# A third exponential chain on the job bank, and the last query block's products begun early, in a fused attention and token-mixing kernel

## The chip, the cores and the metric

The kernel runs on one core of one Trainium2 chip. The metric is the device time in microseconds (us) of one execution. A profiled execution also gives the span from the first to the last instruction, which is about 2 us shorter than the device time, and the mean granted clock of TensorE (1.0 is full speed).

## The reference

```python
x  = A_x                                   # (1, 2048, 640) bf16
xn = layernorm(x)
# multi-head attention: 32 heads of 20, wqkv 640 x 1920, wo 640 x 640
q, k, v = split(xn @ wqkv)
s = concat(softmax(q k^T * 20**-0.5) v) @ wo
# token-mixing MLP over the sequence: F = 1536
u = gelu(einsum("bsd,sf->bdf", layernorm(xn), w1) + b1)
y = (einsum("bdf,fs->bds", u, w2) + b2).transpose(0, 2, 1)
return x + s * silu(y)
```

## The kernel before

The kernel's Python is a planner. It keeps a clock for each engine, with its own estimates of every instruction and transfer, and at each step emits the candidate instruction that it ranks best. What reaches the chip is one fixed order of instructions for each engine, tied together by semaphores.

The softmax is 2048 units of 128x512 scores, which TensorE writes into PSUM banks. ScalarE takes pairs of units from banks (0,1) and (2,3). VectorE takes single units from banks 4 and 5, each with a chain of six instructions. Bank 6 accumulates the value products. Bank 7 is the job bank: QKV, the MLP and the output products pass through it one after the other.

TensorE has slack, and the kernel fills it (797.6 of 865.0 us busy, of which 68.0 us are recorded filler). Filler matmuls go to the job bank when that is empty (`warm_step`), or with zero weights into the accumulator (`warm_acc`). They are there for the sake of TensorE's granted clock. The planner wants at least `WARM_FLOOR` columns of matmul in a window of its own clock; the window's length, 3413 ns, is a constant of the program.

```python
    OP_FROM = (1792.0, 1852.0, 1926.0)   # from which unit on the products of query blocks 0..2 may start
    ACT_GROUPS = ((0, 1), (2, 3))
    DVE_GROUPS = ((4,), (5,))
    DVE_TAIL_GUARD = 3                   # VectorE keeps off the last units of a pass
    LAST_GUARD = 10
    WARM_ACC = 3600.0
    WARM_FLOOR = 3600.0
    QSPLIT = ((0, 256), (256, 256))      # the last pass comes in two halves
# ... class Prog
    DMA_LAT = 2000.0                     # what the planner takes a transfer to need, ns
    def dma(self, fn, ...):
        # ...
        t.fin = self.pipe = max(t.t0 + self.DMA_LAT, self.pipe) + nbytes / self.DMA_RATE
```

The output products need the heads' results transposed. They are stored to a scratch tensor in DRAM, and each query block is loaded back by a transposing load, `oT`. Before the change, the products of the last query block are released in this way (comments are mine):

```python
        for i, (q0, nq) in enumerate(self.QSPLIT[:-1]):
            b0, nb = NB - 4 + q0 // 128, nq // 128
            # epL0: the first half of the last pass has been accumulated and stored
            rq = oTall[NTB - 1] + ("wo", f"epL{i}") + tuple(f"a2_{b}" for b in range(b0, b0 + nb))
            for b in range(b0, b0 + nb):
                add_bank_job(f"op{b}_0", op_steps(b), rq, 30.0, NU - UP)
                add_job(f"res{b}", res_steps(b), (f"op{b}_0", f"op{b}_1", f"x2_{NTB - 1}"), 30.0)
            # ...
        BA, BB = (5, 7), (4, 0)          # fixed banks for the very last products
        def tail_fin(i):
            b = LBS[i]
            steps = op_mms(b, ps(BA[i]), 0, 512, bank_slot[BA[i]], False, True)
            steps += op_mms(b, ps(BB[i], 128), 512, 128, bank_slot[BB[i]], False, True)
            # ...
```

Of the kernel before, what the change touches and what calls it, by code (L numbers as in the profile page):

```python
# [7 lines left out]
ALU = mybir.AluOpType  # L8
# [274 lines left out]
class _Kern:  # L283
# [14 lines left out]
    DVE_GROUPS = ((4,), (5,))  # L298
# [10 lines left out]
    DVE_TAIL_GUARD = 3  # L309
    LAST_GUARD = 10  # L310
    NTMP = 4
# [90 lines left out]
    def schedule(self):  # L402
# [785 lines left out]
        def emit_dchain(chn):  # L1188
            (fn, rd, wr, cost), us, s0, grp = chn.pop(0)
            tk = pr.dve(fn, reads=rd, writes=wr, name=f"dexp{us[0]}", cost=cost)  # L1190
            if not chn:
                dchains.remove(chn)
                dgrp_state[grp] = "free"
                for i, u in enumerate(us):
                    avail.append((tk.fin, u, "d", s0 + i))
# [253 lines left out]
        for i, (q0, nq) in enumerate(self.QSPLIT[:-1]):  # L1449
            b0, nb = NB - 4 + q0 // 128, nq // 128  # L1450
            rq = oTall[NTB - 1] + ("wo", f"epL{i}") + tuple(f"a2_{b}" for b in range(b0, b0 + nb))
            for b in range(b0, b0 + nb):
                add_bank_job(f"op{b}_0", op_steps(b), rq, 30.0, NU - UP)
# [4 lines left out]
        BA, BB = (5, 7), (4, 0)  # L1458

        def tail_fin(i):  # L1460
            b = LBS[i]
            steps = op_mms(b, ps(BA[i]), 0, 512, bank_slot[BA[i]], False, True)
            steps += op_mms(b, ps(BB[i], 128), 512, 128, bank_slot[BB[i]], False, True)
            z = ztmp(i)
            g = regC[:, b, :]
            steps.append(("act", lambda e: e.activation(z[:, 512:640], ps(BB[i], 128), AF.Copy), [bank_slot[BB[i]]],
                          [S_(f"z{i}_1")], f"tz{b}b", ac(128)))
            if i == 0:
                steps.append(("dve", lambda e: e.tensor_tensor(g[:, 0:512], ps(BA[i]), g[:, 0:512], ALU.mult),
                              [bank_slot[BA[i]], S_(f"g{b}")], [S_(f"r{b}_0")], f"tp{b}a", dv(512)))  # L1470
                steps.append(("dve", lambda e: e.tensor_tensor(g[:, 512:640], z[:, 512:640], g[:, 512:640], ALU.mult),
                              [S_(f"z{i}_1"), S_(f"g{b}")], [S_(f"r{b}_1")], f"tp{b}b", dv(128, .52)))
            else:
                steps.append(("act", lambda e: e.activation(z[:, 0:512], ps(BA[i]), AF.Copy), [bank_slot[BA[i]]],
# [9 lines left out]
        for i, b in enumerate(LBS):  # L1484
            rq = oTall[NTB - 1] + ("wo", f"a2_{b}")
            add_job(f"tpa{i}", (lambda bk, i=i, b=b: op_mms(b, ps(BA[i]), 0, 512, bank_slot[BA[i]], True, False) + [
                ("tag", f"tpa{i}")]), rq + (f"bankoff{BA[i]}",), 60.0 + i)
            add_job(f"tpb{i}", (lambda bk, i=i, b=b: op_mms(b, ps(BB[i], 128), 512, 128, bank_slot[BB[i]], True, False) + [
                ("tag", f"tpb{i}")]), rq + (f"bankoff{BB[i]}",), 60.0 + i)
            add_job(f"tfin{i}", (lambda bk, i=i: tail_fin(i)),  # L1490
                    (f"tpa{i}", f"tpb{i}", f"epL{len(self.QSPLIT) - 1}", f"x2_{NTB - 1}"), 10.0 + i)


# [16 lines left out]
        def pe_cands(T):  # L1510
            c = []
            if nxt[0] < NU and unit_ok(nxt[0]):
# [3 lines left out]
                for gi in range(len(self.ACT_GROUPS)):  # L1516
                    grp = self.ACT_GROUPS[(last_grp[0] + 1 + gi) % len(self.ACT_GROUPS)]
                    if grp_state[grp] == "free" and all(fin_bank(b) for b in grp):
# [3 lines left out]
                        while len(us) < n and u < NU and unit_ok(u):  # L1522
                            us.append(u)
                            u += 1
                            while u in taken:
                                u += 1
                        if len(us) < n and u < NU:
# [6 lines left out]
            if dveready[0] and self.DVE_EXP:  # L1534
                for dg in self.DVE_GROUPS:
                    if dgrp_state[dg] == "free" and all(fin_bank(b) for b in dg) and dg[0] not in bank_off and dve_room(dg):
# [22 lines left out]
            if self.WARM:  # L1559
                wb = warm_bank()  # L1560
                if wb is None and acc_ok[0] and pv_pass[0] < LASTP and pr.gate.warm \
                        and (pv_left[0] == UP or all(pv_seen.get((pv_pass[0], g), NB) < NB for g in range(GH))):
# [16 lines left out]
            for j in active:  # L1579
                s = j.steps[j.i]  # L1580
                if s[0] == "pe":
                    c.append((j.prio if pr.gate.warm or not self.WARM else -2.0, pr.ready("pe", s[2], s[3]),
# [24 lines left out]

        def dve_room(dg):
            return dve_pick(dg) is not None

        def take_dve(dg, rows=()):
# [4 lines left out]
            dgrp_state[dg] = "full"  # L1616
            dexp.append((du, dg, dg))
# [6 lines left out]
        def do_st(grp, us):  # L1624
# [9 lines left out]
            if self.DVE_EXP and dveready[0]:  # L1634
                for dg in self.DVE_GROUPS:
                    rows = {units[u][3] for u in lst}
                    if dgrp_state[dg] == "free" and len(lst) + len(dg) <= 4 and all(fin_bank(b) for b in dg) \
                            and dg[0] not in bank_off and dve_pick(dg, rows) is not None \
# [5 lines left out]
        def do_step(j, eng):  # L1644
            s = j.steps[j.i]
            j.i += 1
            if s[0] == "ev":
                n = s[8]
                fn = ev_fn(s, eng)
                cost = ac(n) if eng == "act" else dv(n, 0.55 if s[7].startswith("xTe") else 1.04)  # L1650
                getattr(pr, eng)(fn, reads=s[5], writes=s[6], name=s[7], cost=cost)
# [48 lines left out]
        def warm_acc():  # L1700

            zero = bass.AP(v_sb, voff(H - 1) + 22, [[NB * VB, P], [0, P]])
            new = pv_left[0] == UP
            pe_full(lambda e: e.matmul(ps(AB), zero, wrm_sb[:, P:P + 512], start=new, stop=new),  # L1704
# [100 lines left out]
```

## Time and profile before

Three runs gave 866.85 us (866.6 to 866.88). The prediction shows the busy shares and the groups. Beside them:

| what | before |
|---|---|
| units on ScalarE / VectorE | 1776 / 272 |
| filler matmuls, by their weight loads | 263 (214 have a record of their own, 68.0 us busy) |
| VectorE started later than 80 ns before the previous record's end, 60 to 765 us, summed | 41.0 us |
| end of the last exponential | 855.4 us |
| from there to the end of the span | 9.6 us |
| span of a run with full clock | 865.0 us |

Some matmul records are missing from this trace: it has 5918 weight loads (PEld) and 5828 matmuls. The filler lines have 130 and 133 weight loads for 117 and 97 matmuls.

The view by stretches of time is the one to read for the clock. Its columns are the stretch, its length, then the busy us and the instructions of PE, of PE's weight loads, of VectorE, ScalarE and GpSimd, then the granted clock of TensorE, the DMA share and GB/s. The kernel before:

```profile
765.00:815.00 50.00, 45.54 (x340) 13.55 (x344) 47.15 (x117) 49.94 (x56) 0.00 (x0) 1.00 0.32 86
815.00:850.00 35.00, 32.36 (x332) 12.75 (x337) 32.70 (x83) 35.00 (x39) 0.00 (x0) 1.00 0.15 34
850.00:869.00 19.00, 10.17 (x101) 4.08 (x95) 8.62 (x20) 6.42 (x9) 0.00 (x0) 0.95 0.11 37
```

ScalarE is busy all 35.00 us of the stretch from 815 to 850 us, and TensorE has its full clock (the 0.95 of the last row comes from a half clock that starts at 865.25 us, after the end of the span at 865.0).

### The profile page before, as it was taken

The page shows a single profiled execution, that of the slowest core. Times are in us where ns is not written, and L with a number is a line of the kernel's source. Part 1 is how long each engine was busy: PE and PEld are TensorE (multiplying, and loading weights), DVE is VectorE, ACT ScalarE, POOL GpSimd, SP SyncE. Part 2 cuts the span into 40 slices and gives each one's busy share as a digit, 9 for nine tenths or more (in the row PEclk, how much of TensorE's full clock was granted, in tenths as well). Part 3 has the DMA queues.
Part 4 walks back from the last instruction along what each step waited for, and adds up shares of the span by engine and source line. Part 5 has one row for each costly group of instructions (what it writes and reads, how often), then busy time and mean ns, then how long its engine had stood idle before and what let it go on. Part 6 is the DMA issues. An engine that isn't in the chain of part 4 may idle for free.

```text
span 865.0 us, 16498 instructions
## 1 busy us (share of the span) xinstructions
PE 797.6 (92%) x5828; PEld 256.1 (30%) x5918; DVE 823.6 (95%) x2047; ACT 845.4 (98%) x925; POOL 14.0 (2%) x23
## 2 busy tenths in 40 slices
PE   8899999999999999999999999999899998998997
PEld 5422222222222223222322222222222222232233
DVE  8989999999999999999999999999999999999996
ACT  7899999999999999999999999999999999999996
POOL 3200000000000000000000000000000000000000
PEclk9999999999999999999999999999999999999999
DMA  8141010011010323010013022123312201042111
GB/s 236 48 113 30 9 35 10 16 36 31 11 55 14 77 36 88 11 55 10 16 25 78 23 51 52 25 52 71 67 30 46 47 11 11 3 102 69 41 39 41
DMA packets 123350, 39.32 MB, mean 45 GB/s; under 512 B 84312, under 2 KB 122152, under 8 KB 123272
## 3 DMA queue, kind: packets, MB, share of 16 engines
q1 hardware_dynamic: 123272, 38.27, 19.4%
q8 instruction: 50, 0.82, 0.4%
q14 instruction: 28, 0.23, 0.1%
HBM read 25.88 MB, written 9.83 MB: 41 GB/s over the span
## 4 chain that ended last, share of the span: by engine, by line
ACT 87%; PE 9%; DVE 2%; POOL 1%; issue 1%; ACTq 0%; POOLq 0%
ACT pt_sb L1137 85%; PE ps_all L1109 3%; PE ps_all L1224 1%; ACT zt_sb L843 1%; PE ps_all L755 1%; PE ps_all L879 1%; ACT zt_sb L838 1%; PE ps_all L1704 1%; DVE ew_sb L1177 0%; PE ps_all L683 0%; PE ps_all L722 0%; POOL v_sb L1298 0%; PE ps_all L703 0%; DVE dpt_sb L1183 0%; PE ps_all L658 0%
## 5 line engine op out<-in xcount | busy, mean ns | idle before, releaser
L1137 ACT ACTIVATE pt_sb<-ps_all 128x1024 bf16<-128x1024 f32 x888 | 819.9, 1147 | 3.6 <-PE ps_all L1109 3.0
L1109 PE MATMUL ps_all<-qk_sb 32*128 32x512 bf16 (+1 forms) x2112 | 367.8, 377 | 48.3 <-ACT pt_sb L1137 36.7
L1177 DVE TENSOR_SCALAR ew_sb<-ps_all 128x512 uint16<-128x512 uint16 x272 | 184.2, 684 | 20.7 <-PE ps_all L1109 19.6
L1109 PEld LDWEIGHTS ps_all<-qk_sb 32*128 32x128 bf16 x2112 | 97.1, 91 | 347.0 <-ACT pt_sb L1137 299.9
L1183 DVE SCALAR_TENSOR_TENSOR dpt_sb<-ps_all,el_sb 128x512 uint16<-128x512 f32 x272 | 182.0, 684 | 1.8
L1224 PE MATMUL ps_all<-pt_sb,v_sb 128*32 128x512 bf16 (+1 forms) x1833 | 162.6, 378 | 0.3 <-issue 0.3
L1181 DVE TENSOR_TENSOR el_sb<-ev_sb,el_sb 128x512 bf16<-128x512 bf16 x272 | 111.0, 417 | 1.1
L1182 DVE TENSOR_TENSOR el_sb<-el_sb,ew_sb 128x512 bf16<-128x512 bf16 x272 | 110.2, 417 | 0.9
L1224 PE MATMUL ps_all<-dpt_sb,v_sb 128*32 128x512 bf16 (+1 forms) x279 | 83.7, 379 | 0.0
L810 PE MATMUL ps_all<-regB,regA 128*128 128x128 bf16 (+1 forms) x371 | 75.6, 300 | 2.9 <-issue 1.1
L1178 DVE TENSOR_SCALAR ev_sb<-ew_sb 128x512 bf16<-128x512 uint16 x272 | 75.3, 285 | 2.3
L810 PE MATMUL ps_all<-regC,regA 128*128 128x128 bf16 (+1 forms) x370 | 74.2, 300 | 1.8 <-issue 1.0
L1179 DVE TENSOR_SCALAR el_sb<-ew_sb 128x512 bf16<-128x512 uint16 x272 | 75.1, 284 | 0.0
L722 PE MATMUL ps_all<-xnT_sb,wqk_sb 128*112 128x512 bf16 x200 | 68.2, 405 | 0.4 <-DVE zt_sb L816 0.4
L1224 PEld LDWEIGHTS ps_all<-pt_sb,v_sb 128*32 128x32 bf16 x1833 | 35.4, 94 | 55.6 <-issue 50.2
L1696 PE MATMUL ps_all<-wrm_sb 128*128 128x512 bf16 (+1 forms) x117 | 34.0, 376 | 3.9 <-DVE ps_all L513 2.2
L810 PEld LDWEIGHTS ps_all<-regB,regA 128*128 128x128 bf16 x384 | 25.8, 97 | 39.1 <-issue 24.0
L810 PEld LDWEIGHTS ps_all<-regC,regA 128*128 128x128 bf16 x384 | 25.0, 97 | 39.8 <-issue 28.1
L1704 PE MATMUL ps_all<-wrm_sb,v_sb 128*128 128x512 bf16 x97 | 34.0, 385 | 1.3 <-issue 0.7
L755 PE MATMUL ps_all<-wv_sb,xnT_sb 128*128 128x160 bf16 (+1 forms) x160 | 33.7, 303 | 0.4 <-DVE pk_sb L1030 0.3
L879 PE MATMUL ps_all<-wo_sb,xnT_sb 128*128 128x128 bf16 (+3 forms) x151 | 30.2, 298 | 1.1 <-issue 0.5
L722 PEld LDWEIGHTS ps_all<-xnT_sb,wqk_sb 128*112 128x112 bf16 x200 | 20.7, 127 | 30.5 <-issue 13.4
(89 smaller groups left out, 354.4 us busy)
## 6 DMA issues: line engine op xcount, KB each, us to landing
regA<-in_B_w_dram SPq DMA_DIRECT2D x6, 1024.0 KB
regA<-in_B_w_dram SPq DMA_DIRECT2D x8, 768.0 KB
qkT_scratch_dram<-pk_sb SPq DMA_DIRECT2D x40, 112.0 KB
qk_sb<-qkT_scratch_dram SPq DMA_DIRECT2D x56, 80.0 KB
regA<-in_A_x_dram SPq DMA_DIRECT2D x6, 640.0 KB
on_scratch_dram<-on_sb SPq DMA_DIRECT2D x124, 20.0 KB
out_dram<-regC SPq DMA_DIRECT2D x3, 640.0 KB
wqk_sb<-in_A_wqkv_dram SPq DMA_DIRECT2D x2, 680.0 KB
```

The costliest lines, as they stand in the source:

```text
L722: steps.append(("pe", lambda e, dc=dc: e.matmul(ps_all[0:112, bk * 512:(bk + 1) * 512], wqk_sb[:, dc * 1280 + c0:dc * 1280 + c0 + 112], xn ...
L810: steps.append(("pe", lambda e, k=k: e.matmul(ps(bk, n), wap[:, k, col0:col0 + 128], rows[:, k, c0:c0 + n], start=(k == 0), stop=(k == nk ...
L1109: pr.pe(lambda e, outp=outp, lhsT=lhsT, rhs=rhs, g=g: e.matmul(outp, lhsT, rhs, start=True, stop=True, tile_position=(32 * g, 0)), reads=q ...
L1137: tk = pr.act(lambda e: e.activation(outp, inp, AF.Exp, bias=-self.OFFS * math.log(2.0) / 128.0, scale=math.log(2.0) / 128.0), reads=[bank ...
L1177: (lambda e: e.tensor_scalar(w3, lo, 0x7FFF, None, ALU.bitwise_and), bs, [sw], dv(N)),
L1178: (lambda e: e.tensor_scalar(v_, w_, 1.0 / 256.0, -128.0, ALU.mult, ALU.add), [sw], [sv], dv(N, .26)),
L1179: (lambda e: e.tensor_scalar(l_, w_, a3 / 65536.0, (b3 - 64.0 * a3) / 256.0, ALU.mult, ALU.add), [sw], [sl_], dv(N, .26)),
L1181: (lambda e: e.tensor_tensor(l_, v_, l_, ALU.mult), [sv, sl_], [sl_], dv(N, .52)),
L1182: (lambda e: e.tensor_tensor(l_, l_, w_, ALU.mult), [sl_, sw], [sl_], dv(N, .52)),
L1183: (lambda e: e.scalar_tensor_tensor(o_, zr, -(self.OFFS - 16256.0), l_, ALU.add, ALU.add), bs + [sl_], [S_(f"dpt{s0 + i}") for i in range( ...
L1224: pr.pe(lambda e, outp=outp, lhsT=lhsT, rhs=rhs, k=k, g=g: e.matmul(outp, lhsT, rhs, start=(k == 0), stop=(k == NB - 1), tile_position=(0, ...
L1704: pe_full(lambda e: e.matmul(ps(AB), zero, wrm_sb[:, P:P + 512], start=new, stop=new), [S_("warm"), S_("v_ones")], [sl_acc], "warmz", 512)
```

## The change

The intent has three parts. VectorE may run a third chain on the job bank while no job holds it. The first product of the last query block is split: its first part, over the heads that are done earlier, starts `EARLY = 42` units before the end, and its second part follows when the last heads are in. And the very last products take whichever bank comes free first, in place of four fixed ones. A few planner rules change with them. The core of the diff:

```diff
-    DVE_GROUPS = ((4,), (5,))
+    DVE_GROUPS = ((4,), (5,), (7,))
+    SHARED = (7,)
+    JOB_PRIO = 20.0
+    SHARE_END = 1780
...
-    DVE_TAIL_GUARD = 3
+    DVE_TAIL_GUARD = 12
+    EARLY = 42
...
+            def early(bk):
+                return op_mms(b0, ps(bk), 0, 512, bank_slot[bk], True, False) + [
+                    ("call", lambda: keep(bk)), ("tag", f"opA{b0}")]
...
+            def late(_):
+                bk = kept[1]
+                g = regC[:, b0, 0:512]
+                return op_mms(b0, ps(bk), 0, 512, bank_slot[bk], False, True) + [
...
+            add_bank_job(f"opA{b0}", early, oTall[NTB - 1] + ("wo",), 30.0, NU - self.EARLY)
+            add_job(f"opB{b0}", late, rq + (f"opA{b0}",), 11.0)
+            for b in range(b0 + 1, b0 + nb):
+                add_bank_job(f"op{b}_0", op_steps(b), rq, 30.0, NU - UP)
...
-        BA, BB = (5, 7), (4, 0)
+        tbank = []
...
+        def bank_out(b):
+            bank_off.add(b)
+            tbank.append(b)
+            done.add(f"tbank{len(tbank) - 1}")
...
+        def share_ok(dg):
+            return dg[0] not in self.SHARED or nxt[0] < self.SHARE_END
...
+                if s[3] in ("q", "k"):
+                    cost += 130.0
```

Left out here: the bookkeeping of the shared bank, the rule that a pair's two units come from different row groups, and the filler in the accumulator, which is now also allowed in the last passes.

## The prediction

> **What bounds the kernel now.** I read the page's first part, then its chain of waits, then the groups of instructions, then the timeline of VectorE. Busy shares come first.
>
> ```profile
> PE 797.6 (92%) x5828; PEld 256.1 (30%) x5918; DVE 823.6 (95%) x2047; ACT 845.4 (98%) x925; POOL 14.0 (2%) x23
> ACT 87%; PE 9%; DVE 2%; POOL 1%; issue 1%; ACTq 0%; POOLq 0%
> ```
>
> ScalarE is busy 98% of the span, and 87% of the chain that ended last runs through it. VectorE follows with 95%. The groups say what fills them (line, engine, operation, tiles, shapes, count | busy, mean ns | idle before):
>
> ```profile
> L1137 ACT ACTIVATE pt_sb<-ps_all 128x1024 bf16<-128x1024 f32 x888 | 819.9, 1147 | 3.6 <-PE ps_all L1109 3.0
> L1177 DVE TENSOR_SCALAR ew_sb<-ps_all 128x512 uint16<-128x512 uint16 x272 | 184.2, 684 | 20.7 <-PE ps_all L1109 19.6
> L1696 PE MATMUL ps_all<-wrm_sb 128*128 128x512 bf16 (+1 forms) x117 | 34.0, 376 | 3.9 <-DVE ps_all L513 2.2
> L1704 PE MATMUL ps_all<-wrm_sb,v_sb 128*128 128x512 bf16 x97 | 34.0, 385 | 1.3 <-issue 0.7
> ```
>
> The softmax has 32 heads x 4 query blocks x 16 key blocks = 2048 units of 128x512 scores. ScalarE exponentiates 888 x 2 = 1776 of them, two per instruction; VectorE does the other 272, each by a chain of six instructions. So the two engines share one pool of work, and the end comes when both have emptied it. Some of VectorE's idle time is a wait for scores: 20.7 us before the first instruction of a chain (L1177). TensorE isn't the bound: 34.0 + 34.0 us of its work are filler matmuls (L1696, L1704)[...].
>
> The timeline of VectorE alone shows the bubble (start, duration, line, count; idle before it in brackets):
>
> ```profile
> 379.17 1.28 DVE L1177 TENSOR_SCALAR ew_sb<-ps_all 128x512 uint16<-128x512 uint16 x2
> 380.37 0.48 DVE L1178 TENSOR_SCALAR ev_sb<-ew_sb 128x512 bf16<-128x512 uint16 x2
> 380.77 0.49 DVE L1179 TENSOR_SCALAR el_sb<-ew_sb 128x512 bf16<-128x512 uint16 x2
> ...
> 382.99 0.41 DVE L1182 TENSOR_TENSOR el_sb<-el_sb,ew_sb 128x512 bf16<-128x512 bf16 x1
> 383.32 0.74 DVE L816 TENSOR_SCALAR zt_sb<-ps_all,b1h_sb 128x512 bf16<-128x512 f32 x1
> ...
> 384.31 1.28 DVE L1183 SCALAR_TENSOR_TENSOR dpt_sb<-ps_all,el_sb 128x512 uint16<-128x512 f32 x2
> 386.34 1.29 DVE L1177 TENSOR_SCALAR ew_sb<-ps_all 128x512 uint16<-128x512 uint16 x2 [0.75 <-PE ps_all L1109]
> ```
>
> Both chains walk in step. They release their two PSUM banks together at 385.6 us, and VectorE stands for 0.75 us until TensorE has refilled one. A third chain is meant for this hole.
>
> [...] between 60 and 765 us that wait for scores comes 33 times, 14.0 us in all. [...] The kernel uses four for ScalarE, two for the chains, one to accumulate and one (bank 7) for all jobs[...]. [...] Here most instructions start some 83 ns before the end of the record before them (1611 of 1878 between 60 and 850 us), while 184 start 37 ns after it, which I read as places where no other chain had a step ready. [...] median distance of starts 903 ns, records of 1147 ns.
>
> **The prices.** A unit on ScalarE: the chain view's longest runs are 36.77 us for 40 pairs, thus 0.46 us a unit. A unit on VectorE, by distances of starts in the timeline above: 0.60 + 0.20 + 0.20 + 0.33 + 0.33 + 0.60 = 2.26 us (mean over the trace 2.27). If r us of VectorE stall are turned into work and the end moves forward by x, the extra units are n = (r - x) / 2.27, and x = 0.46 n. Hence n = r / 2.73 and x = 0.168 r.
>
> **Part 1, the third chain on bank 7.** I added up from the trace how much later each VectorE instruction started than 80 ns before the end of the one before it: 47.6 us between 60 and 850 us. Of this 21.5 us are the 184 short bubbles (184 x 117 ns), 24.5 us are 52 longer waits. All of it would buy x = 8.0 us, the ceiling of this part. But the chain may take bank 7 only when no job holds it or is due, and only up to unit 1780 of 2048. From the first matmul of each job to the end of its eviction the bank was held 637 us by 161 jobs after 55 us. Between jobs, up to 765 us, it stood empty 140.6 us in 114 gaps, and 58 of those were under 0.5 us, which is a change of jobs and not free time. With three chains in flight and VectorE's other work between, a chain holds its bank for some 3 x 2.9 = 8.7 us (estimate: 790 us / 272 units = 2.9 us a unit now). About 113 us of usable gap hold some 13 to 20 such chains. Of the 41 us of stall up to 765 us, 7.0 us fall while the job bank was idle. That gives x = 0.168 x 7.0 = 1.2 us. A late job shifts the gaps and a third chain breaks the step of the other two for a while after, so I double it: r = 12 to 14, about 5 extra units, x = 2.1 us. I choose this, knowing that only the 7.0 is counted.
>
> **Part 2, guard and pairing.** Holding VectorE off the last 12 units of a pass, not 3, protects the change of pass against chains that now take longer. Of the 13.5 us by which ScalarE's starts lag 903 ns between 53 and 853 us, only 3.0 lie within 3 us of a pass end. I give it 0. The pairing rule (two units of a pair from different row groups) has nothing to mend in the kernel before: no pair breaks it. The filler that may now go into the accumulator in the last passes adds nothing on the path.
>
> **Part 3, the tail.** The last exponential ends at 855.37 us. Then comes a fixed chain, and after it TensorE's last products:
>
> ```profile
> 855.61 0.54 PE ps_all L879 x2
> 856.14 0.33 PE ps_all L1224 x8
> 856.48 0.66 PE ps_all L879 x8
> ...
> 858.97 1.13 PE ps_all L879 x4
> 860.10 0.39 PE ps_all L884 x2
> 860.49 0.02 issue
> 860.51 0.28 ACT zt_sb L1466
> ```
>
> The last value products (L1224 x8) start at 856.14, 0.6 us after they could, behind output products of the block before. The second last block's first half waits for the fixed bank 7, which is given back only about 858.4, so its five matmuls (L879 x4 and one) run at 858.97, though the timeline has the loads of their inputs issued at 838.4. After the change, five matmuls of 512 columns (about 0.22 us each, 1.1 us) of the first block move to around unit 2006, where fillers ran; the job bank's three tail jobs follow earlier, and the last blocks take whichever bank is released first, so nothing waits for bank 7. I work it out: last value products at 855.6; four VectorE steps (856.53 to 858.06 before) end near 857.5; the closing matmuls of both blocks (L884) by 858.3 and not 860.5; ScalarE's copies 0.28 + 0.28 + 0.59 us, then two VectorE steps of 0.49 end near 860.6 instead of 862.33. The last store then lasts as before (862.36 to 865.0). Gain 1.7 us; I take 1.6, since VectorE may queue.
>
> **Sum.** 866.85 - 2.1 - 1.6 = 863.1 us.
>
> **The rivals.** (a) The bank is the bottleneck and jobs run late: a chain of 8.7 us holds up jobs that queue back to back, the MLP's last jobs slip into the tail, and the time is 866 to 869. For it: bank 7 was held about 80% of the time. Against: jobs get the bank first, and the loan ends at unit 1780, near 750 us. (b) The chain fills nearly all stalls, since a third stream also removes the 37 ns bubbles: with r = 35 to 47 the time is 857.5 to 860. Against: it can be there in only a fifth of the time. (c) TensorE becomes the limit for ScalarE's refills, as filler must go and bursts of four score matmuls grow longer: 13.5 us of lag in ScalarE's starts are already there. If they grew by a third, the gain would vanish: 867. For it: PE shows 9 in almost every slice. Against: 68 us of it are filler. (d) Only the tail moves: 865.3.
>
> **Range and chances.** Part 1 can give 0 to 6, part 3 0.8 to 2.2, rescheduling of ScalarE's feeds -2 to +2. So 858.5 to 866.5. Faster by over 2% would need 17.3 us, twice the ceiling of 8.0 plus the tail; slower by over 2% needs jobs to fail badly, which the priority excludes.
>
> **What would show it.** Chain groups with 275 to 280 units in place of 272 and ScalarE with 3 to 4 pairs fewer; idle before the chain's first instruction near 15 us and not 20.7; ScalarE's last exponential near 853.2; from there to the end 8.0 us in place of 9.6. More than 285 units would show (b); a first instruction still waiting 20 us and unchanged counts (d); a larger idle or larger lag on ScalarE (c); jobs of the MLP after 840 us (a). I'd be wrong above all if the third chain's units come out of the other two chains, so that counts don't rise.

866.85 us less 2.1 for part 1 and 1.6 for part 3 is 863.1 us, a gain of 3.7. That a third chain could only borrow the job bank rests on the kernel's own layout: its PSUM tensor in the listing (`ps_all`, 128 x 4096 f32) makes eight banks of 512 columns, and the other seven are taken. And that the filler keeps the clock up was my assumption, which the trace of before doesn't show. The 0.22 us for a matmul of 512 columns is in that trace: the starts of 259 pairs that follow each other lie 226 ns apart in the median (216 to 227 between the tenth and the ninetieth percentile).

## More of the kernel before

Every run, profiled or not, lists its span and its granted clock. This document uses both.

Any change to the planner's numbers reshuffles the whole order.

## The result

The kernel after took 870.45 us (median of six runs, 867.05 to 873.85), beside 867.11 us (866.6 to 868.61) for six runs of the kernel before on the same chip. The ratio is 1.0035, with a 95% interval of 1.0011 to 1.0059. (Here and below, a ratio is the mean time of one kernel's fast runs over the mean of the other's in the same rounds, so it isn't quite the ratio of the medians.) So it is 0.35% slower, not 0.4% faster. 870.45 lies outside the predicted range of 858.5 to 866.5. The 2% class, "same", was right.

The six runs aren't one number with noise on it:

| device us | 867.05 | 870.07 | 870.23 | 870.67 | 870.79 | 873.85 |
|---|---|---|---|---|---|---|
| span, us | 865.0 | 868.2 | 868.2 | 868.6 | 868.8 | 871.8 |
| granted clock | 0.998 | 0.991 | 0.991 | 0.991 | 0.991 | 0.986 |

The longer the run, the lower its clock. The clock records of the profiles know only full clock and half clock, 1.0 and 0.5. A mean clock c over a span s therefore means 2 x (1 - c) x s us at half clock: 15.6 us in the four middle runs, 3.5 us in the best and 24.4 us in the worst. A straight line through the six gives span = 863.6 + 0.32 x (time at half clock). The kernel before has 33 of its 53 runs (all that were taken beside the experiments) below 2.7 us of half clock, and their mean span is 865.07 us.

The result thus has two parts. At full clock the change gains about 865.0 - 863.6 = 1.4 us, where 3.7 was predicted (863.6 is extrapolated: no run of the kernel after was quite at full clock; the line rests on six points, four of them at one place). And it loses 0.32 x 15.6 = 5.0 us to half clock that the kernel before mostly doesn't have. These sum to 3.6 us, against 3.3 measured.

**The page of the kernel after**, first part, clock row, shares of the chain and the groups of instructions:

```profile
PE 819.9 (94%) x5927; PEld 256.9 (30%) x5927; DVE 822.7 (95%) x2055; ACT 844.9 (97%) x923; POOL 14.0 (2%) x23
...
PEclk9999999999999999999999999999999999999898
...
ACT 80%; PE 13%; DVE 4%; DMA 1%; POOL 1%; issue 1%; SPq 0%; ACTq 0%; DVEq 0%; POOLq 0%
...
L1141 ACT ACTIVATE pt_sb<-ps_all 128x1024 bf16<-128x1024 f32 x888 | 820.8, 1128 | 8.5 <-PE ps_all L1113 8.0
...
L1181 DVE TENSOR_SCALAR ew_sb<-ps_all 128x512 uint16<-128x512 uint16 x273 | 182.8, 682 | 23.5 <-PE ps_all L1113 22.6
...
L1757 PE MATMUL ps_all<-wrm_sb,v_sb 128*128 128x512 bf16 (+1 forms) x233 | 79.3, 387 | 0.8 <-DVE tr_sb L1283 0.8
```

Against the page of before: ScalarE's share of the chain fell from 87 to 80%, PE's rose from 9 to 13%, and a DMA is in it now. ScalarE waits 8.5 us for scores in place of 3.6. VectorE did 273 units in place of 272, and its first chain instruction waits 23.5 us in place of 20.7. The clock row has two dips near the end (a 9 there stands for 90% or more, so full clock). The same stretches as before:

```profile
765.00:815.00 50.00, 47.09 (x342) 14.16 (x340) 47.89 (x119) 49.09 (x54) 0.00 (x0) 1.00 0.33 88
815.00:850.00 35.00, 33.06 (x286) 11.03 (x287) 30.34 (x74) 32.32 (x35) 0.00 (x0) 0.84 0.13 30
850.00:869.00 19.00, 13.59 (x143) 5.38 (x139) 10.33 (x25) 9.15 (x13) 0.00 (x0) 0.86 0.10 35
```

Between 815 and 850 us ScalarE does 35 instructions, where it did 39, and VectorE 74 in place of 83. The clock is 0.84. TensorE issues 286 matmuls in place of 332 and is no less busy for it: each takes longer. What came just before? The timeline of the kernel after (start, duration, engine, line, operation; idle before it in brackets):

```profile
809.29 1.12 SPq L870 DMA_TRANSPOSE xnT_sb<-on_scratch_dram  x1
...
811.81 0.61 PE L1233 MATMUL ps_all<-pt_sb,v_sb 128*32 128x512 bf16 x6
...
813.42 0.39 PE L883 MATMUL ps_all<-wo_sb,xnT_sb 128*128 128x512 bf16 x1 [1.00 <-DMA xnT_sb<-on_scratch_dram]
...
814.17 1.94 ACT L1141 ACTIVATE pt_sb<-ps_all 128x1024 bf16<-128x1024 f32 x2 [0.91 <-PE ps_all L1113]
...
839.11 2.43 SPq L870 DMA_TRANSPOSE xnT_sb<-on_scratch_dram  x2
...
842.99 0.39 PE L883 MATMUL ps_all<-wo_sb,xnT_sb 48*128 48x512 bf16 x1 [0.51 <-DMA xnT_sb<-on_scratch_dram]
843.31 0.39 PE L1113 MATMUL ps_all<-qk_sb 32*128 32x256 bf16 x4
...
846.12 0.60 PE L1113 MATMUL ps_all<-qk_sb 32*128 32x256 bf16 x4
```

Twice an output product (L883) stands at the head of TensorE's queue before its transposed load has landed: 1.00 us at 813.42, the third query block's product, and 0.51 us at 842.99, the early product of the last block. Behind the first, ScalarE ran dry for 0.91 us. In the records the clock is halved from 814.5 to 821.3 and from 845.2 to 852.0 us, 1.1 and 2.2 us after the two waits ended. The last two lines are the same four matmuls before and during the second: 0.39 and 0.60 us.

The kernel before has one such wait, a shorter one, and no half clock behind it:

```profile
814.15 1.12 SPq L866 DMA_TRANSPOSE xnT_sb<-on_scratch_dram  x1
...
816.75 0.39 PE L879 MATMUL ps_all<-wo_sb,xnT_sb 128*128 128x512 bf16 x1 [0.46 <-DMA xnT_sb<-on_scratch_dram]
```

What do the traces show of this clock? The granted value is never anything but 1.0 or 0.5, and its changes lie on a grid of 3.413 us. In the profile of the kernel after 808.96, 6.83, 23.89, 6.83 and 13.65 us lie between one change and the next: 237, 2, 7, 2 and 4 steps. In that of the kernel before the one stretch at full clock lasts 860.16 us, 252 steps. I call a step a window. Over all profiles the stretches at half clock that end within the span last 3.4, 6.8, 10.2, 13.7 or 30.7 us, which is 1, 2, 3, 4 or 9 windows. And the phase changes from run to run: counted from the start of the program, the first record of full clock begins at 5.1 us in the profile of before and at 7.9 us in that of before_early42, whose first 5684 weight loads are the same. How busy TensorE was before a half clock stands under "Rival (c)" below. My reading of one program giving six different times is this: a thin place in its order, with few columns of matmul, costs something only where a window happens to fall on it. It isn't proved. tail_fill below has an example, where one order has a window of 2688 columns with half clock behind it in one run, and a window of 3584 at that place, with full clock, in another.

**The tail** of the kernel after, in the chain of waits:

```profile
860.12 0.33 PE ps_all L1233 x8
860.45 2.42 PE ps_all L883 x12
...
863.63 0.39 PE ps_all L888 x2
```

The last value products (L1233) are followed by twelve output product matmuls in a row, and a few more after them. Before, value products ended at 856.47 and the last product at 860.49, 4.0 us; here it is 860.45 to 864.02, 3.6 us. From the end of the last exponential (859.46) to the end of the span it is 8.7 us, in place of 9.6 us.

### The profile page after: what moved, and what is told of

Read it like the earlier page. It is cut to its first block, busy times and chain, and to the rows that moved or that the text cites. A ratio compares the mean times of both kernels' runs of the same rounds, so it can differ in the third digit from the quotient of the medians.

```text
span 868.2 us, 16784 instructions
## 1 busy us (share of the span) xinstructions
PE 819.9 (94%) x5927; PEld 256.9 (30%) x5927; DVE 822.7 (95%) x2055; ACT 844.9 (97%) x923; POOL 14.0 (2%) x23
## 4 chain that ended last, share of the span: by engine, by line
ACT 80%; PE 13%; DVE 4%; DMA 1%; POOL 1%; issue 1%; SPq 0%; ACTq 0%; DVEq 0%; POOLq 0%
ACT pt_sb L1141 78%; PE ps_all L1113 5%; PE ps_all L1233 2%; PE ps_all L814 1%; PE ps_all L883 1%; PE ps_all L1757 1%; ACT zt_sb L847 1%; PE ps_all L759 1%; ACT zt_sb L842 1%; DVE ew_sb L1181 1%; DMA xnT_sb<-on_scratch_dram 1%; DMA on_scratch_dram<-on_sb 1%; DVE dpt_sb L1187 1%; PE ps_all L687 0%; DVE el_sb L1186 0%
## 5 line engine op out<-in xcount | busy, mean ns | idle before, releaser
L1181 DVE TENSOR_SCALAR ew_sb<-ps_all 128x512 uint16<-128x512 uint16 x273 | 182.8, 682 | 23.5 <-PE ps_all L1113 22.6
L1233 PE MATMUL ps_all<-pt_sb,v_sb 128*32 128x512 bf16 (+1 forms) x1831 | 165.0, 381 | 0.0
L1233 PE MATMUL ps_all<-dpt_sb,v_sb 128*32 128x512 bf16 (+1 forms) x281 | 81.8, 383 | 0.0
L1757 PE MATMUL ps_all<-wrm_sb,v_sb 128*128 128x512 bf16 (+1 forms) x233 | 79.3, 387 | 0.8 <-DVE tr_sb L1283 0.8
L814 PE MATMUL ps_all<-regB,regA 128*128 128x512 bf16 (+1 forms) x384 | 79.4, 303 | 0.3 <-DVE pk_sb L1034 0.2
L814 PE MATMUL ps_all<-regC,regA 128*128 128x128 bf16 (+1 forms) x384 | 77.6, 303 | 0.3
L1233 PEld LDWEIGHTS ps_all<-pt_sb,v_sb 128*32 128x32 bf16 x1831 | 36.3, 95 | 53.0 <-issue 49.2
L883 PE MATMUL ps_all<-wo_sb,xnT_sb 128*128 128x512 bf16 (+3 forms) x160 | 34.6, 310 | 2.0 <-DMA xnT_sb<-on_scratch_dram 1.5
L1757 PEld LDWEIGHTS ps_all<-wrm_sb,v_sb 128*128 128x128 bf16 x233 | 18.8, 98 | 38.2 <-issue 32.8
```

Source lines behind the costliest of these rows:

```text
L814: steps.append(("pe", lambda e, k=k: e.matmul(ps(bk, n), wap[:, k, col0:col0 + 128], rows[:, k, c0:c0 + n], start=(k == 0), stop=(k == nk ...
L1181: (lambda e: e.tensor_scalar(w3, lo, 0x7FFF, None, ALU.bitwise_and), bs, [sw], dv(N)),
L1233: pr.pe(lambda e, outp=outp, lhsT=lhsT, rhs=rhs, k=k, g=g: e.matmul(outp, lhsT, rhs, start=(k == 0), stop=(k == NB - 1), tile_position=(0, ...
L1757: pe_full(lambda e: e.matmul(ps(AB, nq, q0), zero, wrm_sb[:, P:P + nq], start=new, stop=new), [S_("warm"), S_("v_ones")], [sl_acc], "warmz ...
```

## The experiments

Two theories stood at the start. **A**: the early products wait for a load, TensorE starves the other engines and loses its clock. **B**: the third chain does it, by taking the job bank or by disturbing the order. All 17 kernels gave right results. Each was run five or six times. Runs marked slow (one of guard3, one of g3e28) are left out of the ratios, but not of the medians in this table; by fast runs alone guard3 has a median of 869.33 us and g3e28 of 866.17.

| kernel | median us (lowest to highest) | ratio to before, 95% interval |
|---|---|---|
| no_third | 871.85 (869.23 to 880.65) | 1.0068 [1.0036, 1.0100] |
| no_early | 869.06 (867.49 to 869.33) | 1.0017 [1.0005, 1.0029] |
| dma_true | 871.23 (864.54 to 876.64) | 1.0031 [1.0003, 1.0058] |
| third_only | 866.40 (865.84 to 868.07) | 0.9996 [0.9983, 1.0008] |
| guard3 | 870.84 (866.20 to 883.02) | 1.0034 [1.0004, 1.0064] |
| early28 | 868.08 (866.46 to 870.42) | 1.0009 [0.9996, 1.0022] |
| tail_fill | 868.43 (867.57 to 876.84) | 1.0039 [1.0005, 1.0073] |
| qk130 | 868.35 (867.53 to 868.72) | 1.0011 [0.9998, 1.0024] |
| fill38 | 876.88 (867.13 to 879.77) | 1.0086 [1.0047, 1.0125] |
| e28_fill38 | 866.64 (865.77 to 871.59) | 0.9998 [0.9977, 1.0018] |
| before_thin | 866.64 (866.21 to 874.28) | 1.0013 [0.9984, 1.0043] |
| g3e28 | 866.58 (865.49 to 887.28) | 0.9993 [0.9973, 1.0012] |
| before_early42 | 874.76 (871.00 to 878.46) | 1.0074 [1.0045, 1.0104] |
| before_op28 | 866.91 (865.65 to 868.14) | 0.9992 [0.9980, 1.0005] |
| e28f38_dma | 866.39 (865.85 to 867.07) | 0.9985 [0.9973, 0.9997] |
| g3e28_dma | 866.42 (866.34 to 866.69) | 0.9986 [0.9974, 0.9998] |
| g3e28_dma_no3 | 867.58 (867.29 to 869.77) | 1.0002 [0.9989, 1.0016] |

The kernel before took 866.94, 867.25, 867.23, 867.59 and 867.03 us (medians) beside the five submissions.

### First: take the parts apart

**no_third** is the kernel after without the third chain.

```diff
-    DVE_GROUPS = ((4,), (5,), (7,))
-    SHARED = (7,)
+    DVE_GROUPS = ((4,), (5,))
+    SHARED = ()
```

> The changed kernel with only the two old chains, all else as changed. Theory A (the third chain does nothing, the loss is TensorE waiting for the transposed loads and two stretches at half clock): still about 869 to 871, clock near 0.99, a wait of products on the load of about 1 us or more. Theory B (borrowing the job bank costs the time): back to 865 to 866.5, clock 1.0. Theory C (any reshuffle of the static order moves the time by 1 to 2 us): anywhere from 865 to 869 with no half clock.

It stayed slow, at 871.85 us, with half clock in five of six runs, so the third chain isn't needed for the loss. Its only run at full clock had a span of 867.0 us, worse than before at full clock (865.0). The built program gives VectorE only 268 units, where the kernel before has 272. I put this down to the longer guard (12 units in place of 3), which had been put at nothing. So part of this kernel's loss has another cause than that of the kernel after. For B, third_only below says more.

**no_early** is the kernel after with the last block's first product at its old place (the split taken out, the loop over `b0` to `b0 + nb` put back).

> The changed kernel with the first products of the last query block back at their old place. Theory A: the half-clock stretch near 844 us goes, the one near 813 us stays; about 1.5 us less than the changed kernel, so 868 to 869. Theory B: no change against the changed kernel, 870 to 871. Theory C: unpredicted, within 2 us of it.

869.06 us, clock 0.994 to 0.998. That is 1.4 us less than the kernel after, and still 2.1 us more than the kernel before beside it: without early products a good part of the loss stays. Its profile has a wait of 1.9 us on the load of the third query block, and half clock once for 3.4 us after it (816.5 us) and once for 3.4 us far from any load (649.2 us).

**dma_true** tells the planner longer times for the transfers of this path, 3.0 us for the stores and 3.7 us for the loads, each before its bytes. These are estimates: the chain of waits of the kernel after has 2.50 and 3.56 us for two stores, and 4.08 and 2.53 us for two loads, bytes included. Where an expectation below speaks of "true times", it means them.

```diff
+        lat = 3700.0 if name.startswith("oTload") else 3000.0 if name.startswith("onst") else self.DMA_LAT
-        t.fin = self.pipe = max(t.t0 + self.DMA_LAT, self.pipe) + nbytes / self.DMA_RATE
+        t.fin = self.pipe = max(t.t0 + lat, self.pipe) + nbytes / self.DMA_RATE
```

> The changed kernel, but the scheduler is told that the stores of the heads' results and their transposed loads take 3.0 and 3.7 us and not 2.0 us before their bytes, [...]so it places the products after the load. Theory A: no wait of products on loads over 0.3 us, no half clock before the end, clock 0.997 or more, 865 to 867. Theory B: 870 as before, since the third chain is as it was. Theory C: 866 to 870.

A missed its number here: 871.23 us. The runs go from a span of 862.7 (clock 0.998) to 874.8 (0.979). The profile of the 874.8 run has half clock at 537.6 us for 10.2, at 704.9 for 13.7 and at 851.6 for 10.2 us, and still a wait of 0.9 us on a load. So half clock doesn't follow waits on loads alone: before the one at 537.6 us TensorE was busy for 2.93 of 3.40 us and waited for no load. This order has thin places in the middle too. They aren't this edit's own. By the traces, its weight loads are those of the kernel after, in the same order, for the first 5495 of 5927, up to 813 us. The kernel after has the same thin places, and its one profiled run was spared there.

**third_only** is the kernel before with the third chain, the pairing rule, the planner's cost of the q and k evictions and the filler in the last passes, but with the old guard, the old tail and no early products.

```diff
-    DVE_GROUPS = ((4,), (5,))
+    DVE_GROUPS = ((4,), (5,), (7,))
+    SHARED = (7,)
+    JOB_PRIO = 20.0
+    SHARE_END = 1780
...
-        BA, BB = (5, 7), (4, 0)
+        tbank = [5, 4, 7, 0]
```

> The kernel before with only the third chain on the job bank (with the pairing rule and the filler in the accumulator), old guard, old tail. Theory A: as the kernel before within 1 us, 866 to 868, about 273 units on VectorE, since the third chain only takes units from the other two. Theory B: 2 us or more slower than the kernel before, 869 to 871. My prediction's reading (it fills stalls): 864.7.

866.4 us, ratio 0.9996: neither gain nor loss that can be told. So the third chain by itself doesn't bring the loss, and B falls as far as that goes. In its profile, at full clock, the last exponential ends at 855.03 us (855.38 before), and VectorE did 273 units.

### Second: guard, distance and filler

**guard3** undoes the guard alone (`DVE_TAIL_GUARD = 12` to `3`) in the kernel after.

> The changed kernel with the old guard of 3 units. Without the third chain the guard of 12 cost 4 units (268 instead of 272), so the old guard may give the third chain room for more. Theory A (loads and half clock): 273 units again, half-clock stretches in the tail stay, 869 to 871. Theory D (the guard of 12 costs the time): 866 to 867.5 and no half clock.

870.84 us, as slow as the kernel after by the ratios (1.0034 and 1.0035). Its full-clock run had a span of 864.2 us, and its profiled one 873.8 us with half clock at 818.8 us for 10.2 and at 846.1 us for 13.7 us. The guard isn't the cause.

**early28** lets the early products start 28 units before the end in place of 42.

```diff
-    EARLY = 42
+    EARLY = 28
```

> The changed kernel, the first products of the last query block released 28 instead of 42 units before the end, after their loads have landed; the order of work is the same up to unit 2006. Theory A: no wait for the load near 842 us and no half clock after 836 us in the profile; about 1.5 us less than the changed kernel: 868 to 869.5. Rival (the products begun early are free, what hurts lies earlier): unchanged, 870 to 871.

868.08 us, and 864.5 us of span at full clock in the profile. There is no wait for the last block's load any more. The one for the third block's (1.2 us) is still there.

**tail_fill** raises the filler's floor to 4400 columns from unit 1880 on.

```diff
-  short_at(T, self.WARM_FLOOR, ...)
+  short_at(T, (4400.0 if nxt[0] >= 1880 else self.WARM_FLOOR), ...)
```

(`WARM_ACC` gets the same condition; left out here.)

> The changed kernel with more filler matmuls from unit 1880 on (the floor of columns per 3.4 us raised from 3600 to 4400 there), nothing else. Theory A: the clock holds at full speed from 745 us on although the waits for loads remain; 866 to 868.5. If the half clock is only a symptom and the waits are the cost: still 870 or more, as filler adds work to TensorE.

868.43 us as median, but two of six runs have spans above 874. The profile of one shows no half clock from 745 us to the end. But TensorE waits for no load there either, as the order of the tail has changed, so the run doesn't tell more filler from a missing wait. It has half clock at 91.4, 538.5 and 705.8 us instead (3.4, 10.2 and 13.7 us). The edit can't have put it there: it acts from unit 1880 on, and the first 5311 weight loads, up to 786 us, are those of the kernel after in the same order. So one order gives half clock in one run and none in another. By the count explained under "Rival (c)" below, the window from 535.1 us holds 2688 columns here and is followed by half clock; in the profile of the kernel after the windows fall otherwise, and the one from 534.6 us holds 3584.

**qk130** asks how much a mere reshuffle moves the time. It is the kernel before with one planner estimate changed, and no other part of the change.

```diff
+                if s[3] in ("q", "k"):
+                    cost += 130.0
```

> The kernel before with nothing but the changed planning cost of the evictions of queries and keys (130 ns more in the scheduler's clock); it changes no instruction, only the order from the start on. It measures what a mere reshuffle does. Theory C (reshuffling moves the time by 1 to 3 us): 868 to 870. If order alone is harmless: 866.5 to 867.5.

All runs had clock 1.0, and the spans are 865.4 to 866.5 us, where the kernel before has 865.07 us at such a clock. So this reshuffle cost about 1 us, and no difference of that size between two orders can be put down to a part of the change.

### Third: does more filler help, does less hurt?

**fill38** is the kernel after with both floors at 3800, **e28_fill38** the same with `EARLY = 28`, **g3e28** the kernel after with `EARLY = 28` and the guard at 3, **before_thin** the kernel before with less filler.

```diff
-    WARM_ACC = 3600.0
-    WARM_FLOOR = 3600.0
+    WARM_ACC = 3800.0      # fill38 and e28_fill38
+    WARM_FLOOR = 3800.0    # before_thin: 3300.0, and WARM_ACC kept
```

> The changed kernel with a little more filler everywhere: the scheduler keeps 3800 and not 3600 columns in each 3.4 us. Over the ten profiles so far the span is about 865.2 us + 0.31 us for each us at half clock. Theory A (half clock is the loss, from windows too thin): fewer half-clock windows, spread between runs under 4 us, median 866.5 to 868.5. If the half clock were not the loss: 870 or more, since filler only adds work.

> The same with the early products released 28 units before the end, after their loads. Theory A: both thin windows of the tail mended, no half clock before the end in most runs, 865.5 to 867.5, at best 1 us under the kernel before. Rival: as the changed kernel, 869 to 871.

> The kernel before with less filler: 3300 and not 3600 columns kept in each 3.4 us, nothing else. Theory A: half clock now comes to the kernel before as well, several windows, median 868 to 874 and a spread of some us. If the old kernel's clock is safe by its order of work and not by its filler: 865 to 867, no half clock.

> The changed kernel with the old guard of 3 and the early products 28 units before the end: the third chain and the tail without the two parts that hurt by theory A. Expected 865.5 to 868, a profile without half clock near 864.3. If the third chain itself brings thin windows by taking the filler's bank: 868 to 871.

A missed its number for fill38, and instructively. With more filler it came out worse, 876.88 us. (The order is another from 50 us on, so the floor isn't the only difference.) The profile has one wait of 2.8 us on the load, and from 842.2 us on half clock for 30.7 us. While TensorE stood idle for those 2.8 us before a matmul whose input wasn't there, no filler planned behind it ran: the planner, which believes that the input is there, sees no hole to fill. The same floor with the products released 14 units later gave 866.64 us, 10 us less, though one of its six runs still had 0.992 of the clock.

before_thin shows the other half. The kernel before doesn't need the change to fall to half clock. With the floor at 3300 in place of 3600, four of six runs were as before (spans 864.0 to 864.6 us), and two had 872.1 us at 0.985 and 869.9 us at 0.990. The kernel before had no run in 53 with more than 8.7 us of half clock; these two have 26.2 and 17.4. This supports that the filler is the margin of the clock; the order has changed with it, so it isn't proof.

g3e28 had three runs of 863.5 to 864.2 us at full clock, one of 865.0 us at 0.997, one of 868.3 us at 0.991, and one slow (887.28 us, clock 0.964).

### Fourth and fifth: the proof, and a better kernel

By now A was supported by pairs of kernels, but each pair carried the rest of the change. **before_early42** is the kernel before with nothing but the split first product, released 42 units before the end. **before_op28** has the same at 28, and also the third query block's products 16 units later.

```diff
+    EARLY = 42             # before_op28: 28
-    OP_FROM = (1792.0, 1852.0, 1926.0)
+    OP_FROM = (1792.0, 1852.0, 1942.0)   # before_op28 alone
```

> The kernel before with the early products of the last query block alone, released 42 units before the end: no third chain, old guard, old banks; the order is that of the kernel before up to unit 2006. Theory A (the products block TensorE on the transposed load, the window becomes thin, the clock halves): a wait of 0.5 us or more near 842 us, half clock after it in most runs, 868 to 871. If the third chain were needed for the loss: 866 to 867, full clock.

> The kernel before with the early products released 28 units before the end, and the products of the third query block 16 units later than before, so that both come after their loads; nothing else. Theory A: no wait for a load over 0.3 us, full clock to the end in nearly all runs, 866 to 866.7, thus 0.3 to 1.0 us under the kernel before. The prediction's tail term (1.6 us) would give 865.5.

before_early42 took 874.76 us, 7 us more than before, with clocks of 0.980 to 0.992 in all six runs. Its timeline:

```profile
838.65 2.54 SPq L867 DMA_TRANSPOSE xnT_sb<-on_scratch_dram  x2
...
841.24 0.61 PE L880 MATMUL ps_all<-wo_sb,xnT_sb 128*128 128x512 bf16 x1 [1.57 <-DMA xnT_sb<-on_scratch_dram]
...
842.43 1.02 ACT L1138 ACTIVATE pt_sb<-ps_all 128x1024 bf16<-128x1024 f32 x1 [1.47 <-PE ps_all L1110]
...
846.50 0.69 DVE L1178 TENSOR_SCALAR ew_sb<-ps_all 128x512 uint16<-128x512 uint16 x1 [3.09 <-PE ps_all L1110]
```

The loads are issued from 838.65 us on. TensorE comes to the early product, waits 1.57 us for the load, and behind it ScalarE waits 1.47 us for scores and VectorE 3.09 us. By stretches:

```profile
820.00:840.00 20.00, 18.26 (x180) 6.96 (x183) 18.70 (x47) 20.00 (x23) 0.00 (x0) 1.00 0.07 6
840.00:845.00 5.00, 3.47 (x30) 1.06 (x30) 3.37 (x9) 3.00 (x4) 0.00 (x0) 0.57 0.61 181
845.00:850.00 5.00, 4.19 (x44) 1.37 (x40) 3.47 (x11) 4.49 (x5) 0.00 (x0) 0.50 0.00 0
```

ScalarE goes from 20.00 of 20 us to 3.00 of 5 us as the clock falls, and the clock stays at half for 30.7 us. Nothing of the third chain is in this kernel. Early products alone, released at unit 2006, cost more than the whole change did.

before_op28 has no wait on a load at all, and took 866.91 us (0.9992). One of its runs, at 0.999 of the clock, had a span of 863.7 us.

**g3e28_dma** is the kernel after with `DVE_TAIL_GUARD = 3`, `EARLY = 28` and the transfer times of dma_true. **e28f38_dma** keeps the guard of 12 and has both floors at 3800 instead. **g3e28_dma_no3** is g3e28_dma without the third chain.

> The changed kernel with early products at 28 units, 3800 columns of filler kept in each window, and the scheduler told the true times of the stores and transposed loads. Theory A: 865.5 to 866.5, at least four of six runs at full clock, no waits for loads over 0.3 us. If thin windows come from elsewhere too: a median of 867 or more.

> The same with the old guard of 3 and the old filler of 3600. Theory A: full-clock runs near 865.5; some runs with half clock, as the filler's margin is as thin as in the kernel before and the job bank is lent: median 866 to 868.

> The mended version g3e28_dma (old guard, early products at 28 units, true times for stores and loads) with the third chain taken out and nothing else changed. If the third chain gains nothing: within 0.7 us of g3e28_dma, full clock in most runs, 866 to 867. If it earns the 0.15% (by its 2 units and by filling bubbles): 867.3 to 869.

Both beat the kernel before by a little, with intervals that exclude 1: 0.9985 and 0.9986. They also beat the kernel after, by 4 us of the medians. The gain over before is flattered: the kernel before had half clock in several runs, and 867.59 us is its highest median of five. Against its spans at full clock (865.07) g3e28_dma has 0.5 to 0.9 us, no more than qk130 moved. g3e28_dma is the steadiest kernel, 866.34 to 866.69 us, with clocks of 0.998 to 1.000 in every run. One row of its groups, then its chain of waits:

```profile
L1182 DVE TENSOR_SCALAR ew_sb<-ps_all 128x512 uint16<-128x512 uint16 x273 | 183.6, 684 | 19.5 <-PE ps_all L1114 18.0
```

```profile
856.21 0.33 PE ps_all L1234 x8
856.54 2.31 PE ps_all L884 x12
858.86 0.23 PE ps_all L889
```

The chain's first instruction waits 19.5 us (20.7 before), and the tail from the last exponential is 9.1 us (9.6). The twelve product matmuls that remain behind the value products take 2.31 us: in the built program they write banks that the last units give back only with their exponentials.

Without the third chain the span at full clock is 865.3 to 865.6 us, with it 864.2 to 864.6. It does 271 units without and 273 with. So the third chain is worth about 1.0 us here. qk130 moved as much by a reshuffle, so this is a measured difference of two orders and not a proof of its cause.

## Why the prediction was wrong

**What bounds the kernel: right.** ScalarE and VectorE share one pool of units and their end sets the time. It is the reason why a TensorE that stands still costs anything at all.

**Part 3, the place of the early products: the step that failed.** The prediction said that five matmuls "of the first block move to around unit 2006, where fillers ran", and counted only their gain. It had itself quoted the issue of their loads at 838.4 us, and never compared the landing with the time of unit 2006, which is 838 to 841 us. The kernel after has two loads there, one behind the other (`--critical`: start, us, what):

```profile
839.11 1.12 SPq L870
840.41 2.53 DMA xnT_sb<-on_scratch_dram
```

From its own issue to the first matmul on it the first load takes 2.6 us (839.11 to 841.76), the second too (840.41 to 842.99), and so does the load of before_early42 (838.65 to 841.24). The planner reckons 2.0 us and 131072 / 220 = 596 ns for the bytes, the same 2.6 us. So in the last block the loads last as planned and are issued too late: from the first store to the first load the plan of before_early42 has 3.65 us (read from the planner), the trace 5.29 (833.36 to 838.65). The third block's load in the kernel after was itself longer, 4.1 us (809.29 to 813.42), and in guard3 5.0 (812.03 to 817.05), where the kernel before has 2.6 (814.15 to 816.75). So the products came up on TensorE before their inputs, and it stood idle before them, for 0.51 us in the kernel after and 1.57 us in before_early42. Four pairs of kernels show what the release costs. In each pair the weight loads are the same, in the same order, for the first 5667 to 5714 of some 5900, up to 837 to 841 us:

| pair (medians of fast runs, us) | release at 42 units | at 28 units, or none |
|---|---|---|
| kernel after / early28 | 870.45 | 868.08 |
| guard3 / g3e28 | 869.33 | 866.17 |
| fill38 / e28_fill38 | 876.88 | 866.64 |
| before_early42 / before | 874.76 | 867.59 |

All four go the same way, by 2.4 to 10.2 us. The first three are the change of one constant; in the fourth the kernel before doesn't have the split either. They aren't the whole loss: beside the kernel before, early28 is still 0.8 us over and no_early 2.1. Both still wait for the third block's load (1.2 and 1.9 us) and have the thin places in the middle. What each of these two costs in the six runs of the result isn't shown: only one run was profiled, and its half clock before the end lies behind the two waits.

**Rival (c), the filler: misread.** The prediction set against it that "68 us of it are filler", as though filler were free time. before_thin, with two of six runs at 0.985 and 0.990, speaks for its being the margin of the clock. I counted the columns of the matmuls that start in each window, a row- or column-tiled matmul for a quarter (as the planner does; no run tests that weight), with missing matmul records put in by their weight loads. The two windows before the half clock of the kernel after hold 2816 and 2752, the thinnest of the kernel before 3104, and the planner holds itself to 3600. But another window of the kernel after, from 462.9 us, holds 2560 and kept the full clock. Over all 19 profiles 21 windows at full clock hold under 3000, and 14 of them are followed by half clock; of the other 4376 (from 60 us on, up to 9 us before the end), five are. So thinness goes with half clock, but my count doesn't give a sharp limit. Busy time doesn't either. TensorE was busy for 2.04 of 3.40 us in the window before the first half clock of the kernel after (811.1 to 814.5 us) and for 2.89 in that before the second (841.8 to 845.2), while the window from 462.9 us, with 2.71, kept the full clock. Nor did one busy window bring the clock back: TensorE was busy for all 3.40 us from 814.5 us, and another window at half clock followed. The rival's 867 counted the longer waits for scores; what it lacked was the clock.

**Part 1, the third chain: mis-sized against the kernel before.** Predicted were r = 12 to 14 us of stall turned into work, 5 extra units and 2.1 us. VectorE's stall from 60 to 765 us is 41.0 us before and 41.7 after: in sum r is nothing. The short bubbles did shrink, from 171 to 125, 46 x 117 ns = 5.4 us. The long waits grew by 5.0 us, from 15.5 to 20.5. Among them is the wait that the chain was meant to fill. The waits of the kernel before and of the kernel after in that stretch (instruction <- releaser: us, times, longest us):

```profile
DVE ew_sb L1177 <- PE ps_all L1109: 14.0, 33, 0.8
```

```profile
DVE ew_sb L1181 <- PE ps_all L1113: 17.6, 31, 1.1
```

In the built program the third chain starts 12 times (13 to 20 were predicted) and the other two do 135 and 126 units in place of 138 and 134. The prediction's last sentence named just this: that its units "come out of the other two chains". The bank was held 7.5 us for a chain in the plan, 8.7 had been estimated. So the ceiling and the number of starts were about right.

But the kernel before isn't the only thing to compare with. no_third lacks the chain and has the rest of the change: 268 units and 51.6 us of stall, where the kernel after has 273 and 41.7. That is five units and 9.9 us, near what was predicted. With the guard at 3 (g3e28_dma_no3 and g3e28_dma) it is two units. This speaks for a chain that does turn stall into work, while the rest of the change, which the sum put at nothing, takes it away again: the guard, and the new order (qk130, without a third chain, has 45.1 us of stall). As each of these kernels is also another order, it isn't shown. Why the other chains wait longer for scores is not settled. More filler isn't the reason: by weight loads it went from 263 matmuls to 272 (233 in the accumulator, L1757, and 39 in the job bank, L1748). It moved from the job bank into the accumulator, where 133 were before, and no run changed this alone.

**Part 2, the guard: 0 was right only beside the third chain.** guard3 and the kernel after agree (ratios 1.0034 and 1.0035, 273 units each). Without the third chain the guard of 12 goes with 268 units (no_third) and the guard of 3 with 271 (g3e28_dma_no3, which differs in other things too).

**The tail: right in its mechanism, too large.** 1.6 us were taken. At full clock or near it, the stretch from the last exponential to the end is 8.3 us in e28f38_dma and 9.1 in g3e28_dma, in place of 9.6: 0.5 to 1.3 us. The working let the products of both last blocks end by 858.3 us. They still ran behind the value products, 2.31 us for twelve.

**The sum, as it came out.** -1.4 us at full clock in place of -3.7, and +5.0 us by the clock in place of none: +3.6 us by this sum, +3.3 by the medians.

**The range** had -2 to +2 us for "rescheduling of ScalarE's feeds", which was to cover such things. A reshuffle alone moves about 1 us (qk130), so that was a fair size, but for orders that keep the clock. A lost clock cost 0.32 us for each us at half rate by the line through the six runs, and up to 30.7 us of it came at once. The range was also narrower than its own parts: 0 to 6, 0.8 to 2.2 and -2 to +2 us add up to 856.7 to 868.1. The result lies outside that too.

**What stays open.** What TensorE must do in a window to keep its clock: no count of mine draws the line. Why the half clock of before_early42 and fill38 lasts 30.7 us and doesn't recover, though TensorE is busy in it (in before_early42 for 9.53 of the 10 us from 850 us on). Which of the 1.0 us in g3e28_dma is due to the third chain and which to the order. How much of the loss in the result the thin places in the middle cost, and whether the third chain or the moved filler made them.

## What to carry to other kernels

Release a piece of work by the measured landing of its input, with all that its issue waits for, not by the plan's estimate of it: matmuls that came 0.51 to 1.57 us too early left TensorE idle for that time here, with no filler or other matmul run in their place. Don't count filler as slack before a run with less of it has shown the clock (two of six runs of before_thin had 0.985 and 0.990 of it): look at the clock of every run, and when one program's times scatter, set the span against the time at half clock before asking what the change did. And before crediting 1 us to a part of a change in a planned order, make one edit that means nothing and see how far that moves the time.
